# Queries and keys of batches 1 to 3: head-pair loads and 32x32 VectorE transposes in place of 64-column loads, TensorE and DMA transposes

## The chip, the cores and the metric

The kernel runs on one core of one Trainium2 chip. The metric is the device time of one execution in microseconds (us), lower is better; the figure compared is the median of several runs.

## What is computed

Four batches, 8 heads, 768 tokens, head size 64. Each chunk of 32 query tokens sees 8 memory keys and a window of up to 56 keys (16 before, its own 32, 8 after). The attention output, with heads joined to 512 columns, goes through a gated feed-forward layer of width 1536.

```python
for c in range(nc):                              # 24 chunks of 32 tokens
    q_c   = q[:, :, c_start:c_end]
    k_ctx = k[:, :, l_start:r_end]; v_ctx = v[:, :, l_start:r_end]
    k_full = np.concatenate([mem_k, k_ctx], axis=2)
    v_full = np.concatenate([mem_v, v_ctx], axis=2)
    scores = scale * np.matmul(q_c, k_full.transpose(0, 1, 3, 2))
    a = softmax(scores)                          # row maximum taken off first
    out[:, :, c_start:c_end] = np.matmul(a, v_full)
x = out.transpose(0, 2, 1, 3).reshape(3072, 512)
y = (np.maximum(x @ w_gate, 0) * (x @ w_val)) @ w_out
```

## The kernel before, in words

The work is cut into 24 tiles `a` of 128 tokens (six per batch). A tile needs its queries `qT` and its batch's keys `kT` with the head dimension on the partitions. `scores` (L286) makes one 64-column score block for each head and chunk; `row_max`, `subtract`, `row_sum`, `reciprocal`, `normalise` run on VectorE (DVE) and `exponent` on ScalarE (ACT); the weights are transposed (`p_t`, L343, on TensorE; from tile 18 on by a DMA transpose, L351), multiplied with the values (`values`, L357) and copied into `xT` (`x_copy`). The feed-forward layer runs over blocks of 2 or 4 tiles (`BLOCKS`, L51): `first` (L390) makes a gate and a value product for each of 12 slices of the width, `relu` (ACT) and `gate` (DVE) join them, `second` (L416) multiplies with the output weights and `store` writes out.

Queries and keys arrive in three ways. Batch 0 is loaded by `load_pair` (two tokens a descriptor) and transposed on TensorE (`pair_t`, L221; `pair_copy`). Tiles 6 to 11 are loaded by `load_qk` (L239: 128 tokens on the partitions, runs of 64 numbers), transposed on TensorE by `qk_t` (L260) and copied out by `qk_copy`. Tiles 12 to 23 (`LATE_QK`, L55) are loaded the same way and transposed by a DMA that SyncE (SP) issues, `qk_transfer` (L266): queries straight into `qT`, keys into `k_t`, from where `qk_copy` spreads them into `kT`. Values of batches 1 to 3 go into `v_bd` by `load_v_rows` (L170), and the memory rows by `mem_rows` (L152), all cast on the way by DMAs that GpSimd (POOL) issues.

The order of the instructions on each engine is fixed when the kernel is built: every operation has a key, a cost per engine, dependencies, a priority and the buffers it takes and gives (`room`), and `schedule` (L649) plays the engines through once, gives each engine the first ready operation by priority and emits them in that order. Feed-forward matmuls have the last priority and fill TensorE; `pace` (L145) holds the attention of a tile back until the feed-forward work has come to a given slice. Loads go out in the order of the list `loads` on POOL. Of the eight PSUM banks the feed-forward tiles and the value shifts take four (`fps`), a score tile two (`sps`), and all transposes and value products share two (`aps`).

Of the kernel before, what the change touches and what calls it, by code (L numbers as in the profile page):

```python
# [9 lines left out]
F32 = mybir.dt.float32  # L10
# [9 lines left out]
def kernel(  # L20
# [30 lines left out]
    BLOCKS = [2, 2, 4, 4, 4, 4, 4]  # L51
    GROUPS = [(0, 2), (2, 6), (6, 9), (9, 12)]
    BAND0 = 48

    LATE_QK, LATE_P = 12, 18  # L55
# [5 lines left out]
    ldpool = ctx.enter_context(tc.tile_pool(name="ldpool", bufs=18))  # L61
# [4 lines left out]
    ktpool = ctx.enter_context(tc.tile_pool(name="ktpool", bufs=3))  # L66
# [3 lines left out]
    fps = ctx.enter_context(tc.tile_pool(name="fps", bufs=4, space=bass.MemoryType.PSUM))  # L70
    sps = ctx.enter_context(tc.tile_pool(name="sps", bufs=1, space=bass.MemoryType.PSUM))
    aps = ctx.enter_context(tc.tile_pool(name="aps", bufs=2, space=bass.MemoryType.PSUM))
# [25 lines left out]
    v_n = {}  # L98
    qk_p = {(i, r): const.tile([128, H, 2 * D], BF16, name=f"qk_p_{i}_{r}") for i in range(2) for r in range(TPB // 2)}
# [40 lines left out]
    def mem_keys_t():  # L140
        TMP["kmem"] = aps.tile([128, B * HP * NMEM], F32, tag="aps", name="kmem_ps")
        nc.tensor.transpose(TMP["kmem"], kmem_f.rearrange("p a d -> p (a d)"), ident_f)
# [43 lines left out]
    def load_v_tile(t):  # L186
        v_n[t] = ldpool.tile([128, H, D], F16, tag="qk_b", name="v_n")
        nc.gpsimd.dma_start(
            v_n[t],
            bass.AP(tensor=v.tensor, offset=v[0, 0, 128 * t, 0].offset,  # L190
                    ap=[[D, 128], [S * D, H], [1, D]]))
# [29 lines left out]
    def pair_t(r, i, j):  # L221
        ps = TMP["pair", r, i, j] = aps.tile([128, HP, 128], BF16, tag="aps", name="qk_ps")
        for h in range(H):
            p = D * (h % 2)
            nc.tensor.transpose(ps[p:p + D, h // 2, :], qk_p[i, r][:, h, D * j:D * j + D], ident_b)  # L225
# [13 lines left out]
    def load_qk(a, i):  # L239
        b, t = divmod(a, TPB)  # L240
        x = (q, k)[i]
        qk_b[a, i] = ldpool.tile([128, H, D], BF16, tag="qk_b", name="qk_b")
        nc.gpsimd.dma_start(  # L243
            qk_b[a, i],
            bass.AP(tensor=x.tensor, offset=x[b, 0, 128 * t, 0].offset,
                    ap=[[D, 128], [S * D, H], [1, D]]))

    def new_batch(b):
        qT[b] = kvpool.tile([128, HP, S], BF16, name="qT")
        kT[b] = kvpool.tile([128, HP, NCH, KW], BF16, name="kT")  # L250
        src = kmemT[:, b]
# [3 lines left out]
                    ap=[src.ap[0], [NMEM, HP], [0, NCH], [1, NMEM]]))  # L255
# [4 lines left out]
    def qk_t(a, i):  # L260
        ps = TMP["qk", a, i] = aps.tile([128, HP, 128], BF16, tag="aps", name="qk_ps")
        x = qk_b.pop((a, i))
        for hp in range(HP):
            nc.tensor.transpose(ps[:, hp, :], x[:, 2 * hp:2 * hp + 2, :].rearrange("p h d -> p (h d)"), ident_b)  # L264

    def qk_transfer(a, i):  # L266
        b, t = divmod(a, TPB)
        if i == 0:
            o = qT[b][:, :, 128 * t:128 * t + 128]
        else:  # L270
            o = TMP["qk", a, i] = ktpool.tile([128, HP, 128], BF16, name="k_t")
        nc.sync.dma_start(o, qk_b.pop((a, i)).rearrange("p h d -> p (h d)"), transpose=True)

    def qk_copy(a, i, eng):
        b, t = divmod(a, TPB)
        ps = TMP.pop(("qk", a, i))
        if i == 0:
            copy(eng, qT[b][:, :, 128 * t:128 * t + 128], ps)
        else:
            o = kT[b][:, :, 4 * t:4 * t + 4, :]  # L280
            copy(eng,
                 bass.AP(tensor=o.tensor, offset=o.offset,
                         ap=[o.ap[0], [NCH * KW, HP], [KW, 4], [16 + NMEM, 2], [1, 16]]),
                 ps.rearrange("p h (c x s) -> p h c x s", c=4, x=2))

    def scores(a):  # L286
        b, t = divmod(a, TPB)
        s = sps.tile([128, 2, 512], F32, name="s_ps")
        keys = kT[b].rearrange("p h c s -> p h (c s)")
        for h2 in range(HP):  # L290
            m, par = h2 % 2, h2 // 2
            for g in range(4):
                c = 4 * t + g
                lo, hi = max(KW * c - 16, 0), min(KW * c + 48, NCH * KW)
                o0 = 64 * (2 * m + par) + lo - (KW * c - 16)
                for r in range(2):
                    d = slice(D * r, D * r + D)
                    nc.tensor.matmul(s[CH * g:CH * g + CH, r, o0:o0 + hi - lo],  # L298
                                     lhsT=qT[b][d, h2, CH * c:CH * c + CH],
                                     rhs=keys[d, h2, lo:hi], start=True, stop=True)  # L300
        S_ps[a] = s.rearrange("p a (h s) -> p a h s", s=64)[:, :, 0:HP, :]

    def row_max(a):
# [6 lines left out]
        SM[a, "mx"] = smpool.tile([128, 2, HP], F32, name="mx")  # L310
        nc.vector.reduce_max(SM[a, "mx"], s4, axis=AX.X)  # L311

    def subtract(a):
        mx = SM.pop((a, "mx"))
        SM[a, "dif"] = smpool.tile([128, HP, 2, 64], F32, name="dif")
        mx_b = bass.AP(tensor=mx.tensor, offset=mx.offset,
                       ap=[mx.ap[0], [HP, 2], [2, 2], [1, 2], [0, 64]])
        nc.vector.tensor_tensor(out=SM[a, "dif"].rearrange("p (m r) a s -> p r m a s", r=2),  # L318
                                in0=S_ps.pop(a).rearrange("p r (m a) s -> p r m a s", a=2),
                                in1=mx_b, op=ALU.subtract)  # L320
# [103 lines left out]
    def store(blk, t, c, eng):  # L424
# [12 lines left out]
    room = {"aps": 2, "sps": 1, "fps": 4, "mx": 2, "dif": 2, "p": 2, "sm": 2, "rinv": 2, "pn": 3, "kt": 3, "pT": 6,  # L437
            "qk": 18, "xT": 2, "gv": 2, "gr": 3, "o": 3, "kv": 2}
# [11 lines left out]
    def psum16(n):  # L450
# [8 lines left out]
    op("vmem_f", {"DVE": 0.55}, lambda e: nc.vector.memset(vmem_f, 0.0), prio=(-8,), after=["warm"])  # L459
    op("kml", {"SP": 1.4}, lambda e: mem_load(), prio=(-9,))  # L460
# [3 lines left out]
    op("kmt", {"PE": 0.25}, lambda e: mem_keys_t(), [("kml", 1.8), "if"], prio=(-5,), take=["aps"])  # L464
    op("kmc", {"ACT": 0.35}, lambda e: nc.scalar.copy(kmemT.rearrange("p b h m -> p (b h m)"), TMP.pop("kmem")),
       ["kmt"], prio=(-5,), give=["aps"])
    op("vm0", {"DVE": 0.5}, lambda e: nc.vector.tensor_copy(vmem_0, vmem_f), [("vml", 1.8)], prio=(-3,))
    for b in range(B):
        op(("new", b), {"DVE": 0.4}, lambda e, b=b: new_batch(b), ["kmc"], take=["kv"],
           prio=(-4.5,) if b == 0 else (1, TPB * b - 2, 0), after=[("t", TPB * b - 2, 0)] if b else [])  # L470


    AHEAD = 4

    def pace(a):
        blk = block_of[a]
        m = NDC * (a - starts[blk]) // BLOCKS[blk] - (AHEAD if a >= LATE_P else 0)
        if blk < 2:
            return []
        return [("f", blk - 1, m, 0)] if m >= 0 else [("f", blk - 2, m + NDC, 0)]  # L480


    ISSUE, LAND, SLACK, LAND_P = 1.4, 6.0, 8.0, 3.0

    def pace_t(a):
        return [("s", a - 4)]

    for a in range(NT):
        b, t = divmod(a, TPB)
        last = t == TPB - 1  # L490
        for i in (1, 0):
            if b == 0:
                if t % 2 == 0:
                    for j in range(2):
                        op(("t", a + j, i), {"PE": 0.3}, lambda e, a=a, i=i, j=j: pair_t(a // 2, i, j),
                           [("pl", a // 2, i), "ib", ("new", b)], (1, a - i, -2 + j), ["aps"])
                        op(("tc", a + j, i), psum16(HP * 128), lambda e, a=a, i=i, j=j: pair_copy(a // 2, i, j, engine[e]),
                           [("t", a + j, i)], (1, a - i, -2 + j), (), ["aps"])
                continue
            if a >= LATE_QK:  # L500
                op(("t", a, i), {"SP": ISSUE}, lambda e, a=a, i=i: qk_transfer(a, i),
                   [(("qk", a, i), SLACK), ("new", b)],
                   (1, a - i, 0), ["kt"] if i else [], [("qk", LAND)], pace_t(a))
                if i:
                    op(("tc", a, i), {"DVE": (0.2, 0.29), "ACT": (0.52, 0.62)}, lambda e, a=a, i=i: qk_copy(a, i, engine[e]),
                       [(("t", a, i), LAND)], (1, a - i, 0), (), ["kt"])
                continue
            op(("t", a, i), {"PE": 0.24}, lambda e, a=a, i=i: qk_t(a, i), [("qk", a, i), "ib", ("new", b)],
               (1, a - i, 0), ["aps"], ["qk"], pace(max(a - i, 0)))
            op(("tc", a, i), psum16(HP * 128), lambda e, a=a, i=i: qk_copy(a, i, engine[e]), [("t", a, i)],  # L510
               (1, a - i, 0), (), ["aps"])
        op(("s", a), {"PE": 0.36}, lambda e, a=a: scores(a),
           [(("t", a, 0), LAND) if a >= LATE_QK else ("tc", a, 0), ("tc", a, 1)]
           + ([] if last else [("tc", a + 1, 1)] if b or t % 2 == 0 else [("tc", a + 1, 1), ("tc", a + 2, 1)])
           + ([("tc", a ^ 1, 0)] if b == 0 else []), (1, a, 1), ["sps"],
           ["kv"] if last else [], [("s", a - 1)] if a else [])
# [13 lines left out]
        if b == 0:  # L530
            for c0 in (4 * t, 4 * t + 2):
                need = {c // 4 for c in (c0, c0 + 1)} | {max(c0 - 1, 0) // 4, min(c0 + 2, NCH - 1) // 4}
                gone = ([t - 1] if c0 % 4 == 0 and t else []) + ([t] if c0 == NCH - 2 else [])
                op(("sh", c0), {"PE": 0.4}, lambda e, c0=c0: shift(c0), [("vn", n) for n in sorted(need)] + ["ident"],
                   (1, a, 7.5), ["fps"], ["qk"] * len(gone), [("s", t)])
# [13 lines left out]
    seq = [(blk, m) for g0, g1 in GROUPS for blk in range(2) for m in range(g0, g1)]  # L549
    seq += [(0, None), (1, None)]  # L550
    for blk in range(2, len(BLOCKS)):
# [228 lines left out]
```

## Time and profile before

| | |
|---|---|
| median of 3 runs | 251.47 us (249.82 to 252.72) |
| the profiled execution | 254.24 us, of which the span of the instructions is 252.5 us |
| TensorE (PE) busy | 234.0 us, 93% of the span; mean granted clock 0.986 |
| VectorE / ScalarE / GpSimd busy | 131.3 / 115.0 / 90.7 us |
| chain that ended last | PE 79%, DMA 12%, DVE 4%, ACT 3% |
| DMA packets | 116285, of them 107297 under 512 B |

The profile is one execution of the program, taken by the hardware profiler. A line of a group names the source line, the engine, the operation, what is written and read, how often, and the busy time. A line of the timeline or of the chain gives start and length in us; a bracket at its end gives the idle time of that engine ahead of the instruction and what ended it. The time of an execution is a little longer than the span (1.7 us here), for what lies ahead of the first and behind the last instruction.

### The profile page before, as it was taken

What the parts mean: (1) busy time and instruction counts of PE and PEld (TensorE: products, weight loads), DVE (VectorE), ACT (ScalarE), POOL (GpSimd) and SP (SyncE); (2) the same over time, 40 slices, a digit from 0 to 9 for tenths busy, and PEclk for the clock granted to TensorE, in tenths of its full rate; (3) what the DMA queues carried; (4) which work ended last, traced back from release to release, by engine and by line L of the source; (5) the groups of instructions that cost most, each with busy time, mean ns of one, the idle gap of its engine ahead of it and who ended that gap; (6) DMA issues with size and microseconds to landing.
All of it is one profiled execution on the core that took longest, in us unless ns stands there. A gap on an engine that the chain in (4) does not pass through costs nothing.

```text
span 252.5 us, 6081 instructions
## 1 busy us (share of the span) xinstructions
PE 234.0 (93%) x2529; PEld 128.7 (51%) x2529; DVE 131.3 (52%) x245; ACT 115.0 (46%) x250; POOL 90.7 (36%) x105
## 2 busy tenths in 40 slices
PE   1869999999899999799999949999999999999994
PEld 0647887884445555345444424455444544444443
DVE  2462657985158886588543817964049340133400
ACT  2856757763236555356334444543153531333212
POOL 8975899605179950298450060000000000000000
PEclk9999999999999999999999976999999999999999
DMA  7999999999999999999999999222221101300022
GB/s 79 174 179 203 201 84 130 204 156 97 176 203 139 140 135 86 123 211 136 123 116 123 122 138 169 42 44 41 86 83 23 21 0 54 116 1 0 0 85 84
DMA packets 116285, 27.32 MB, mean 108 GB/s; under 512 B 107297, under 2 KB 113185, under 8 KB 116257
## 3 DMA queue, kind: packets, MB, share of 16 engines
q0 software_dynamic: 94368, 16.42, 113.4%
q1 hardware_dynamic: 21888, 10.51, 24.3%
q8 instruction: 20, 0.33, 0.6%
q14 instruction: 9, 0.07, 0.1%
HBM read 32.06 MB, written 6.29 MB: 152 GB/s over the span
## 4 chain that ended last, share of the span: by engine, by line
PE 79%; DMA 12%; DVE 4%; ACT 3%; issue 1%; POOL 0%; SPq 0%; ACTq 0%; POOLq 0%
PE v_ps L396 25%; PE g_ps L396 25%; PE out_ps L421 18%; DMA k_t<-qk_b 9%; PE s_ps L298 2%; PE xT_ps L377 2%; DMA qk_p<-in_q_dram 2%; PE xT_ps L370 2%; PE vs_ps L204 1%; PE qk_ps L225 1%; PE pT_ps L347 1%; DVE mx L311 1%; DVE dif L318 1%; PE qk_ps L264 1%; PE xT_ps L363 1%
## 5 line engine op out<-in xcount | busy, mean ns | idle before, releaser
L408 DVE TENSOR_TENSOR gvT<-v_ps,g_relu 128x512 f16<-128x512 f32 (+1 forms) x84 | 51.3, 611 | 51.9 <-PE v_ps L396 48.9
L396 PE MATMUL g_ps<-xT,w_gate_sb 128*128 128x512 f16 (+1 forms) x336 | 77.4, 353 | 0.8 <-ACT xT L78 0.8
L396 PE MATMUL v_ps<-xT,w_val_sb 128*128 128x512 f16 (+1 forms) x336 | 77.8, 355 | 0.0
L402 ACT ACTIVATE g_relu<-g_ps 128x512 f16<-128x512 f32 (+1 forms) x84 | 45.0, 535 | 56.2 <-PE g_ps L396 55.9
L421 PE MATMUL out_ps<-w_out_sb,gvT 128*128 128x512 f16 (+2 forms) x300 | 64.9, 371 | 0.0
L396 PEld LDWEIGHTS <-w_gate_sb 128*128 128x128 f16 x336 | 31.7, 99 | 28.3 <-issue 2.0
L396 PEld LDWEIGHTS <-w_val_sb 128*128 128x128 f16 x336 | 31.7, 99 | 27.2 <-issue 1.5
L421 PEld LDWEIGHTS <-gvT 128*128 128x128 f16 x300 | 28.2, 98 | 31.3
L78 ACT COPY o_sb<-out_ps 128x512 f32<-128x512 f32 (+2 forms) x25 | 14.1, 565 | 36.4 <-PE out_ps L421 32.5
L311 DVE TENSOR_REDUCE mx<-s_ps 128x8 f32<-128x512 f32 x24 | 16.4, 683 | 18.7 <-PE s_ps L298 18.2
L326 ACT ACTIVATE p_exp<-dif 128x256 f16<-128x256 f32 (+2 forms) x72 | 19.6, 336 | 10.7 <-DVE dif L318 10.5
L243 POOL DMA_DIRECT2D qk_b<-in_k_dram x18 | 16.4, 911 | 14.4 <-issue 8.0
L330 DVE TENSOR_REDUCE sm<-p_exp 128x8 f32<-128x512 f16 x24 | 16.3, 681 | 9.2 <-ACT p_exp L326 9.0
L156 POOL DMA_DIRECT2D v_bd<-vmem x16 | 10.1, 637 | 28.6 <-DMA v_bd<-in_v_dram 27.4
L243 POOL DMA_DIRECT2D qk_b<-in_q_dram x18 | 16.4, 909 | 3.8 <-issue 2.5
L341 DVE TENSOR_TENSOR p_n<-p_exp,rinv 128x512 f16<-128x512 f16 x24 | 16.5, 687 | 0.4
L318 DVE TENSOR_TENSOR dif<-s_ps,mx 128x512 f32<-128x512 f32 x24 | 16.5, 686 | 0.4
L173 POOL DMA_DIRECT2D v_bd<-in_v_dram x7 | 13.9, 1996 | 5.2 <-issue 3.7
L298 PE MATMUL s_ps<-kT,qT 64*32 64x64 bf16 (+2 forms) x768 | 8.6, 199 | 5.7 <-ACT kT L78 3.3
L298 PEld LDWEIGHTS <-qT 64*32 64x32 bf16 x768 | 5.3, 92 | 14.0 <-issue 11.8
L78 ACT CAST xT<-xT_ps 128x512 f16<-128x512 f32 x14 | 8.2, 586 | 8.5 <-PE xT_ps L377 4.5
L377 PEld LDWEIGHTS <-v_bd 128*128 128x128 f16 x288 | 9.4, 97 | 3.6 <-issue 0.3
(52 smaller groups left out, 159.8 us busy)
## 6 DMA issues: line engine op xcount, KB each, us to landing
out_dram<-o_sb SPq DMA_DIRECT2D x23, 256.0 KB
v_bd<-in_v_dram POOLq DMA_DIRECT2D x5, 672.0 KB, 18.0
qk_b<-in_k_dram POOLq DMA_DIRECT2D x18, 128.0 KB, 7.5
qk_b<-in_q_dram POOLq DMA_DIRECT2D x18, 128.0 KB, 7.8
w_out_sb<-in_moe_w_out_dram POOLq DMA_DIRECT2D x2, 768.0 KB, 11.6
qk_p<-in_k_dram POOLq DMA_DIRECT2D x3, 256.0 KB, 6.1
qk_p<-in_q_dram POOLq DMA_DIRECT2D x3, 256.0 KB, 6.5
v_n<-in_v_dram POOLq DMA_DIRECT2D x6, 128.0 KB, 6.5
```

The lines of the kernel that those rows point to most:

```text
L78: nc.scalar.copy(o, i)
L243: nc.gpsimd.dma_start(qk_b[a, i], bass.AP(tensor=x.tensor, offset=x[b, 0, 128 * t, 0].offset, ap=[[D, 128], [S * D, H], [1, D]]))
L298: nc.tensor.matmul(s[CH * g:CH * g + CH, r, o0:o0 + hi - lo], lhsT=qT[b][d, h2, CH * c:CH * c + CH], rhs=keys[d, h2, lo:hi], start=True, s ...
L311: nc.vector.reduce_max(SM[a, "mx"], s4, axis=AX.X)
L318: nc.vector.tensor_tensor(out=SM[a, "dif"].rearrange("p (m r) a s -> p r m a s", r=2), in0=S_ps.pop(a).rearrange("p r (m a) s -> p r m a s ...
L326: nc.scalar.activation(p[:, :, :, s0:s0 + k1 - k0], dif[:, :, :, k0:k1], ACT.Exp, scale=SCALE)
L330: nc.vector.reduce_sum(SM[a, "sm"], SM[a, "p"], axis=AX.X)
L341: nc.vector.tensor_tensor(out=P_n[a], in0=SM.pop((a, "p")), in1=rinv_b, op=ALU.mult)
L396: nc.tensor.matmul(ps, lhsT=w[:, f, 128 * m:128 * m + 128], rhs=xTs[blk][:, f, :], start=(f == 0), stop=(f == NFC - 1))
L402: nc.scalar.activation(st["r", m], st.pop((0, m)), ACT.Relu)
L408: nc.vector.tensor_tensor(out=st["gv"][:, m, :], in0=st.pop((1, m)), in1=st.pop(("r", m)), op=ALU.mult)
L421: nc.tensor.matmul(st["o", t, c], lhsT=st["gv"][:, m, 128 * t:128 * t + 128], rhs=w_out_sb[:, m, c[0]:c[1]], start=(m == 0), stop=(m == ND ...
```

## The change

Batch 0 keeps its way. For batches 1 to 3:

- Loads. Per batch, query or key: four DMAs of 384 descriptors (one for each pair of heads, onto 32 partitions) in place of six of 1024; a descriptor reads four tokens, 256 numbers. They sit in whole-batch buffers, three of them, one shared with batch 0's values.
- Transposes. Per batch eight `keys_t` (128 partitions, 384 elements each) and six `queries_t` (512 elements) on DVE, in 32x32 blocks, straight into `kT` and `qT`. The TensorE transposes and copies of tiles 6 to 11, the 24 DMA transposes and the copies from `k_t` are gone.
- Head halves. A head's 64 numbers now lie as two halves of 32 on the same partitions, so `scores` makes two accumulating products of 32 rows for each head and chunk: 64 matmuls a tile in place of 32, each head pair into a PSUM bank of its own. Memory keys of batches 1 to 3 are loaded apart (four small DMAs), zero-filled and transposed on DVE once (`mem_keys_b`).
- PSUM. Scores take four banks (batch 0 uses the upper two for its transposes), feed-forward three (before four), weight transposes and value products one (before two).
- Blocks. [2, 2, 2, 4, 4, 4, 4, 2] in place of [2, 2, 4, 4, 4, 4, 4].
- Order. `pace` works from an estimated clock; the last group of gate weights is loaded behind the last query pair and value tile of batch 0; two of the four zero fills of `v_bd[1]` move from POOL to DVE ahead of everything else; key and query loads of batch 1 stand behind the output weights, and those of batches 2 and 3 behind the values of the batch before.

```diff
-    BLOCKS = [2, 2, 4, 4, 4, 4, 4]
+    BLOCKS = [2, 2, 2, 4, 4, 4, 4, 2]
-    ldpool = ctx.enter_context(tc.tile_pool(name="ldpool", bufs=18))
+    ldpool = ctx.enter_context(tc.tile_pool(name="ldpool", bufs=3))
-    fps = ctx.enter_context(tc.tile_pool(name="fps", bufs=4, space=bass.MemoryType.PSUM))
+    fps = ctx.enter_context(tc.tile_pool(name="fps", bufs=3, space=bass.MemoryType.PSUM))
-    aps = ctx.enter_context(tc.tile_pool(name="aps", bufs=2, space=bass.MemoryType.PSUM))
+    aps = ctx.enter_context(tc.tile_pool(name="aps", bufs=1, space=bass.MemoryType.PSUM))
+    s_all = sps.tile([128, 4, 512], F32, name="s_ps")
...
-        nc.gpsimd.dma_start(
-            qk_b[a, i],
-            bass.AP(tensor=x.tensor, offset=x[b, 0, 128 * t, 0].offset,
-                    ap=[[D, 128], [S * D, H], [1, D]]))
+        nc.gpsimd.dma_start(
+            qk_b[b, i][CH * hg:CH * hg + CH],
+            bass.AP(tensor=x.tensor, offset=x[b, 2 * hg, 0, 0].offset,
+                    ap=[[TPP * D, CH], [128 * D, 2 * TPB], [1, TPP * D]]))
...
+    def queries_t(b, r, h):
+        n = TPB * h + 2 * r
+        o = qT[b][:, 2 * h, 256 * r:256 * r + 256]
+        nc.vector.transpose(
+            bass.AP(tensor=o.tensor, offset=o.offset, ap=[o.ap[0], [128, 2], [1, TPP], [S, 2], [TPP, CH]]),
+            qk_b[b, 0][:, n:n + 2].rearrange("p n j d -> p (n j d)"))
+
+    def keys_t(b, j, e):
+        o = kT[b][:, e, :, j:KW]
+        nc.vector.transpose(
+            bass.AP(tensor=o.tensor, offset=o.offset,
+                    ap=[o.ap[0], [2 * NCH * KW, 2], [KW, NCH], [16 + NMEM, 2], [TPP, 16 // TPP]]),
+            qk_b[b, 1][:, :, j, CH * e:CH * e + CH])
...
-    def qk_transfer(a, i):
-        nc.sync.dma_start(o, qk_b.pop((a, i)).rearrange("p h d -> p (h d)"), transpose=True)
...
+        S_ps[a] = s_all[:, :, 0:128].rearrange("p g (h s) -> p g h s", s=64)
+        for h in range(2):
+            for e in range(2):
+                for hg in range(4):
+                    d = slice(CH * hg, CH * hg + CH)
+                    for g in range(4):
...
+                        nc.tensor.matmul(s_all[CH * g:CH * g + CH, hg, o0:o0 + hi - lo],
+                                         lhsT=qT[b][d, 2 * h + e, CH * c:CH * c + CH],
+                                         rhs=keys[d, 2 * h + e, lo:hi], start=(e == 0), stop=(e == 1))
...
+    for hp in range(2):
+        op(("z", 1, hp), {"DVE": 1.7}, lambda e, hp=hp: zero(nc.vector, v_bd[1], hp), prio=(-7.5, hp), after=["vmem_f"])
...
+    for hg in range(4):
+        load(("mk", hg), 208, 0.2, lambda hg=hg: mem_keys(hg), ["kmb0"])
     for i in range(2):
         load(("wo", i), 768, 4.1, lambda i=i: load_out(i))
+    load_qk_op(1, 1)
+    load_qk_op(1, 0)
```

## The prediction

> **What bounds the kernel now.** I read the page first, for shares; then the chain that ended last, for where time passes that is no matrix work; then the timeline around those places, for prices.
>
> ```profile
> PE 234.0 (93%) x2529; PEld 128.7 (51%) x2529; DVE 131.3 (52%) x245; ACT 115.0 (46%) x250; POOL 90.7 (36%) x105
> ...
> PE 79%; DMA 12%; DVE 4%; ACT 3%; issue 1%; POOL 0%; SPq 0%; ACTq 0%; POOLq 0%
> ```
>
> TensorE is the bound, with little left: 18.5 us of the span without a matmul. About 9 of them lie in the first 20 us (loads and the first softmax) and 3.3 behind the last matmul. What the change aims at is most of the rest, waits for keys that a DMA transposes. The chain around 140 us, columns start, length, what:
>
> ```profile
> 136.70 12.23 DMA k_t<-qk_b
> ...
> 148.95 0.63 ACT kT L78
> ...
> 149.62 0.39 PE s_ps L298 x22
> 150.01 1.82 PE v_ps L396 x4
> 151.83 1.71 PE g_ps L396 x4
> 153.54 0.43 PE xT_ps L377 x16
> 153.97 1.62 PE v_ps L396 x4
> ```
>
> One key transpose takes 12.2 us to land, its copy ends at 149.58, and only then do the scores go on. Afterwards three feed-forward groups take 1.82, 1.71 and 1.62 us where the usual one takes 0.86: the clock had fallen.
>
> ```profile
> 150.00:160.00 10.00, 10.00 (x111) 4.07 (x111) 8.25 (x16) 5.92 (x16) 0.00 (x0) 0.73 1.19 126
> ```
>
> In this stretch the granted clock (third from the end) is 0.73, DVE busy 8.25 of 10. The timeline gives the idle time ahead of the scores (in brackets) there and at two earlier places:
>
> ```profile
> 107.39 0.29 PE L298 MATMUL s_ps<-kT,qT 64*32 64x64 bf16 x26 [1.54 <-DVE kT L80]
> ...
> 110.69 0.32 PE L298 MATMUL s_ps<-kT,qT 64*32 64x64 bf16 x32 [0.49 <-DVE dif L318]
> ```
> ```profile
> 149.62 0.39 PE L298 MATMUL s_ps<-kT,qT 64*32 64x64 bf16 x26 [3.35 <-ACT kT L78]
> ```
>
> **The change, part by part.** The sum is made against the profiled execution, 254.24 us (span 252.5 and 1.7 around it). It lies 2.8 above the median of 251.47; the difference found below is taken off the median.
>
> *Waits on DMA transposes: gone.* 1.54 + 0.49 + 3.35 = 5.4 us idle, and at the lower clock 0.96 + 0.85 + 0.76 = 2.6 us: -8.0. What is late next is under landing, below. The other executions may not all pay the 2.6, so the gain against the median may be 5.4.
>
> *TensorE transposes of tiles 6 to 11: gone.* Twelve groups of four; one stands between groups that start at 89.42 and 89.65, so 0.23 us each: -2.8. Their PSUM copies go too (ACT 6 qT and kT copies at about 0.6 each are off the path).
>
> *Scores of 18 tiles: 64 matmuls in place of 32.* A block of 32 now lasts 0.31 us with matmuls of 0.19, so its starts span 0.12 us, 3.9 ns apart; 0.24 us pass until the next group starts. [...] Upper bound: the starts stay 3.9 ns apart, 64 need 0.25, and 18 x 0.12 = +2.2. I take +2.2, since 3.9 is the only distance that the trace shows. [...]
>
> *One more block of two.* Groups with 256 columns start 0.435 us apart (48.44 to 48.88), with 512 0.86: 48 more of the former against 24 fewer of the latter, 20.9 - 20.7 = +0.2. Twelve more relu and gate pairs (0.39 and 0.42 us) lie beside matmuls.
>
> *DVE.* Added: 24 `keys_t` of 384 elements and 18 `queries_t` of 512. The trace shows no such operation. Nearest rows: a 16-bit SBUF copy of 512 elements 0.29 us (lower), a tensor operation on 512 at full length 0.69, one every 0.60 (upper, keys by size 0.47). I take the upper, since a transpose streams one element after another like those: 24 x 0.47 + 18 x 0.60 = 22 us. With two zero fills (1.6 each from 0.485 for 512), a zero fill of 1024 (1.0) and one transpose, less some ten copies, DVE rises from 131 to about 155 us. [...]
> Does it fit? In the emitted order the key transposes of each batch stand mostly where TensorE multiplies with the output weights (5 to 10 us without a gate). Adding DVE's starts between successive gates, no stretch needs over 1.3 us more on DVE than on TensorE. But feed-forward has three PSUM banks, not four. A value product's bank is free about 0.17 + 0.69 us after its end, while the product that needs it starts one group (0.86) and a half behind: some 0.8 us of slack where there was 1.7, about one DVE operation of 0.69 or one tile's three exponentials (0.81). Some of the 48 gates that fall beside attention will meet both. I take ten times 0.15 us, +1.5 (bounds 0, if the order always fits; +6, if one gate in four loses 0.5 us).
>
> *One bank for weight transposes and value products* makes transposing, copying, multiplying, copying of a tile a chain of 0.23 + 0.6 + 0.4 + 0.7 = 1.9 us against 7.4 us between tiles: hidden by feed-forward groups, except in the start.
>
> *Start.* Scores of tiles 2 and 3 and two value shifts (12 matmuls, 1.49 us at the low clock) move ahead of the first feed-forward group, into idle times of 1.43 and 0.67 us; that is work done earlier, but the second value product waits for the first's copy (+0.6). The zero fills on DVE end at about 4.7, so the first memory-key transpose starts 0.8 later, still ahead of the first keys at 6.1. Together 0 (bounds -2, if the clock rises sooner, +2).
>
> *Landing.* POOL saves two fills of 1.34 us. On its queue, memory keys (four issues at about 0.65), output weights, then eight loads of batch 1 and the values follow. An output weight half (0.75 MB) landed every 3.7 us (49.8 and 53.5); batch 1's keys, as many bytes, stand right behind both. From about 38 us: 43, 47, keys 51, queries 55, values 69 (before: 67.0). The first `keys_t` stands on DVE behind the gate of the 22nd of 24 small slices, by the order 49 to 51 us; what waits behind it are the last three gates, and TensorE behind these. The queries are needed by about 56, the values at some 71 (before, the product stood at 67.66, just behind their landing). Likewise the memory-key transpose holds the gates behind it if its loads land after 37.8 (I get 37 to 39). I take +1.5 (bounds 0 and +5). Batches 2 and 3 are ahead: 36 loads of 1024 descriptors become 24 of 384, so the queue carries some 27000 packets fewer of its 94368.
>
> Sum: -8.0 - 2.8 + 2.2 + 0.2 + 1.5 + 1.5 = -5.4, or 248.8 for such an execution and 246.1 for the median. Since the median may lack part of the 2.6, I give 246.5.
>
> **Rivals.**
> *A. The order doesn't fit DVE (slower).* If a transpose costs twice what I took (0.94 and 1.2, a reason could be that it writes in steps of four tokens), DVE has 22 us more. The eight key transposes then last 7.5 us and outlast the output stretch of 5.2; the gates behind them come late and three banks give no cover. Following the order, TensorE loses about 5 us at 1.5 times the price and 14 at twice: -5.4 + 14 = +8.6, 260. It is slower than before from about 1.5 times on. For it: DVE is already busy 8.7 of 10 in dense stretches. Against it: full-length operations on this engine all sit at 0.60 to 0.69.
> *B. Batch 1 lands late.* If the loads need as long as those issued at 45 us in the trace of before (22 us), keys land at 59 and TensorE stands some 6 us more, with a clock that falls again (2.6): 246.5 + 7 = 253, no change. For: DMA engines are at 9 tenths in all slices up to 158 us. Against: in the trace that was behind 1.3 MB of short value runs, here it is ahead of them.
> [...]
> *D. The waits were hidden anyway.* If other executions pay only half of them, -1 to -2: 250.
>
> **How the numbers follow.** Forecast (243 to 249): 0.45. C: 0.15. D: 0.12. B: 0.13. A: 0.15, half of it beyond 256. A measurement of this kernel can tell about 1%, here 2.5 us. Faster by over 1% (under 249): 0.45 + 0.15 and a little of D, 0.62. Within 1%: D and half of B, 0.18. Slower: A and the rest of B, 0.20. The range reaches from C's upper end, 240.5, to between B and A, 256; the likeliest case alone 243 to 249.
>
> **What would show it.** Right: no key transposes on SP, no idle above 1 us ahead of the scores between 75 and 170 us, granted clock near 1.00 throughout, transposes on DVE at 0.55 and 0.69 us, a score block's starts 0.25 us long. Wrong: idle of DVE ahead of its first `keys_t` or memory-key transpose (landing), feed-forward matmuls waiting for DVE or ACT (banks), transposes above 0.8 us (A), or an end of the first two blocks later than 57 us (start).

## The result

| kernel | median, us | range, us | runs | ratio to before (95%) |
|---|---|---|---|---|
| before | 252.09 | 249.82 to 252.72 | 4 | |
| after | 263.37 | 262.58 to 265.94 | 4 | 1.048 (1.038 to 1.059) |

The change makes the kernel 11 us slower; 246.5 was forecast, with 256 as the upper end. In the profiled execution (265.94 us, span 264.2) TensorE is busy 238.1 us and idle 26.1, where it was 234.0 and 18.5 before. The table of the experiments gives medians without the executions that took over 1.5% longer than the fastest of the same kernel; the profiled executions of before, e5, e7 and e12 are such longer ones.

The page of after, its shares, the chain that ended last, and two groups (busy us, mean ns of one):

```profile
PE 238.1 (90%) x3153; PEld 141.2 (53%) x3153; DVE 171.1 (65%) x294; ACT 109.3 (41%) x247; POOL 73.5 (28%) x95
...
PE 77%; DVE 15%; issue 4%; ACT 2%; DMA 2%; DVEq 0%; POOLq 0%
...
L281 DVE STREAM_TRANSPOSE qT<-qk_b 128x512 bf16<-128x512 bf16 x18 | 22.7, 1315 | 0.0
L287 DVE STREAM_TRANSPOSE kT<-qk_b 128x384 bf16<-128x384 bf16 x24 | 22.1, 1034 | 0.0
```

DMA has left the chain (12% to 2%), as meant; DVE has taken its place (4% to 15%). The 42 transposes need 44.8 us, where 22 were forecast. The groups of DVE by shape hold a third kind of transpose, the one of the memory keys, whose destination is plain:

```profile
L258 DVE STREAM_TRANSPOSE kmem<-qk_p 128x512 bf16<-128x512 bf16 x1 | 0.7, 702 | 0.0
```

The same 512 elements take 0.702 us there and 1.315 where every fourth element is written. The waits of TensorE, by what ended them (us in total, times, longest):

```profile
PE s_ps L323 <- issue: 3.9, 2, 2.4
PE g_ps L427 <- DVE gvT L439: 3.0, 5, 0.9
PE s_ps L323 <- DVE qT L281: 2.1, 2, 1.2
PE s_ps L235 <- ACT kT L78: 1.4, 1, 1.4
PE s_ps L235 <- ACT qT L78: 1.4, 1, 1.4
PE s_ps L235 <- DVE dif L343: 1.4, 1, 1.4
```

None of these was in the trace of before at such a size. Three kinds are to be told apart: waits for DVE (second, third row), waits inside score blocks for nothing that the profile shows (first), and waits of the pair transposes at the start (the last three). The stretch from 150 us, shown for before with a clock of 0.73, now has the full clock and a full DVE (columns behind the time: length, TensorE, weight loads, DVE, ScalarE, GpSimd, each with its instructions, clock, DMA share, GB/s):

```profile
150.00:160.00 10.00, 8.02 (x115) 3.92 (x114) 10.00 (x15) 3.34 (x6) 0.00 (x0) 1.00 0.01 2
```

DVE is busy 10.00 of 10 us and TensorE 8.02. The chain there:

```profile
152.40 1.04 DVE kT L287
153.44 0.46 DVE gvT L439
153.90 2.46 DVE kT L287 x3
156.36 0.03 issue
156.40 0.72 DVE gvT L439
157.11 1.79 DVE kT L287 x2
```

Between two gates stand one to three key transposes; the gate that frees a feed-forward bank comes when they are done.

Last, a score block and the group behind it, from the timelines of before and of after:

```profile
91.47 0.31 PE L298 MATMUL s_ps<-kT,qT 64*32 64x64 bf16 x32
91.71 0.40 PE L347 MATMUL pT_ps<-band,p_n 128*128 128x128 f16 x4
```
```profile
99.71 0.68 PE L323 MATMUL s_ps<-kT,qT 32*32 32x64 bf16 x64
100.32 1.04 PE L427 MATMUL v_ps<-xT,w_val_sb 128*128 128x512 f16 x4
```

The next group starts 0.61 us behind the block's start; before, with 32 matmuls, it was 0.24. That is 0.37 us a tile, three times the 0.12 of the forecast. The records of the single matmuls of this block of after show where it goes: the first 31 start 3.3 ns apart, then 0.12 us pass with one more start in it, and from the 33rd on they start 8.3 ns apart, 0.48 us from the first start to the last.

### The profile page after: what moved, and what is told of

It reads as the page before. It is cut to its first block, busy times and chain, and to the rows that moved or that the text cites. A ratio compares the mean times of both kernels' runs of the same rounds, so it can differ in the third digit from the quotient of the medians.

```text
span 264.2 us, 7340 instructions
## 1 busy us (share of the span) xinstructions
PE 238.1 (90%) x3153; PEld 141.2 (53%) x3153; DVE 171.1 (65%) x294; ACT 109.3 (41%) x247; POOL 73.5 (28%) x95
## 4 chain that ended last, share of the span: by engine, by line
PE 77%; DVE 15%; issue 4%; ACT 2%; DMA 2%; DVEq 0%; POOLq 0%
PE out_ps L452 21%; PE g_ps L427 21%; PE v_ps L427 20%; DVE kT L287 4%; DVE qT L281 4%; PE s_ps L323 3%; PE xT_ps L408 3%; DVE gvT L439 2%; PE s_ps L235 2%; DMA qk_p<-in_k_dram 2%; PE pT_ps L378 2%; PE vs_ps L214 2%; DVE mx L335 1%; PE xT_ps L401 1%; ACT kT L78 1%
## 5 line engine op out<-in xcount | busy, mean ns | idle before, releaser
L439 DVE TENSOR_TENSOR gvT<-v_ps,g_relu 128x256 f16<-128x256 f32 (+1 forms) x96 | 53.4, 557 | 47.5 <-PE v_ps L427 33.7
L427 PE MATMUL g_ps<-xT,w_gate_sb 128*128 128x256 f16 (+1 forms) x384 | 78.5, 327 | 3.2 <-DVE gvT L439 3.0
L427 PE MATMUL v_ps<-xT,w_val_sb 128*128 128x256 f16 (+1 forms) x384 | 78.6, 327 | 0.0
L433 ACT ACTIVATE g_relu<-g_ps 128x256 f16<-128x256 f32 (+1 forms) x96 | 47.0, 489 | 65.0 <-PE g_ps L427 64.8
L427 PEld LDWEIGHTS <-w_gate_sb 128*128 128x128 f16 x384 | 36.6, 98 | 29.9 <-issue 6.1
L281 DVE STREAM_TRANSPOSE qT<-qk_b 128x512 bf16<-128x512 bf16 x18 | 22.7, 1315 | 0.0
L287 DVE STREAM_TRANSPOSE kT<-qk_b 128x384 bf16<-128x384 bf16 x24 | 22.1, 1034 | 0.0
L323 PE MATMUL s_ps<-kT,qT 32*32 32x64 bf16 (+2 forms) x1152 | 12.4, 196 | 7.0 <-issue 3.9
L323 PEld LDWEIGHTS <-qT 32*32 32x32 bf16 x1152 | 9.9, 87 | 14.3 <-issue 10.6
L264 POOL DMA_DIRECT2D qk_b<-in_q_dram x12 | 7.3, 612 | 21.1 <-DMA v_bd<-in_v_dram 8.6
```

The costliest lines, as they stand in the source:

```text
L281: nc.vector.transpose(bass.AP(tensor=o.tensor, offset=o.offset, ap=[o.ap[0], [128, 2], [1, TPP], [S, 2], [TPP, CH]]), qk_b[b, 0][:, n:n + ...
L287: nc.vector.transpose(bass.AP(tensor=o.tensor, offset=o.offset, ap=[o.ap[0], [2 * NCH * KW, 2], [KW, NCH], [16 + NMEM, 2], [TPP, 16 // TPP]]),
L323: nc.tensor.matmul(s_all[CH * g:CH * g + CH, hg, o0:o0 + hi - lo], lhsT=qT[b][d, 2 * h + e, CH * c:CH * c + CH], rhs=keys[d, 2 * h + e, lo ...
L427: nc.tensor.matmul(ps, lhsT=w[:, f, 128 * m:128 * m + 128], rhs=xTs[blk][:, f, :], start=(f == 0), stop=(f == NFC - 1))
L433: nc.scalar.activation(st["r", m], st.pop((0, m)), ACT.Relu)
L439: nc.vector.tensor_tensor(out=st["gv"][:, m, :], in0=st.pop((1, m)), in1=st.pop(("r", m)), op=ALU.mult)
```

## Experiments

Theory: three parts of the change cost time. The transposes write in steps of four tokens, at twice the price (my rival A); the second half of the scores costs 0.37 us a tile and more; scores and pair transposes of batch 0 are cut from one PSUM tile, and wait for one another. Rivals: the transposes were hidden, and scores and start are all; or the planner's order is at fault, which was made with half of the price; or the waits for DMA transposes were no loss.

| run | median, us | before beside it | ratio to before (95%) |
|---|---|---|---|
| e1_runs_of_8 | 257.50 | 251.67 | 1.021 (1.008 to 1.034) |
| e2_half_scores | 259.50 | 251.67 | 1.029 (1.019 to 1.040) |
| e3_own_banks | 260.65 | 251.67 | 1.036 (1.024 to 1.048) |
| e4_before_all_pe | 251.96 | 251.67 | 1.001 (0.997 to 1.005) |
| e5_halves_apart | 261.96 | 251.55 | 1.040 (1.033 to 1.047) |
| e6_three_undone | 245.88 | 251.55 | 0.975 (0.969 to 0.982) |
| e7_best | 257.14 | 251.55 | 1.019 (1.012 to 1.025) |
| e8_one_issue | 250.87 | 251.31 | 0.999 (0.994 to 1.003) |
| e9_true_costs | 264.55 | 251.31 | 1.054 (1.046 to 1.062) |
| e10_batch1_pe | 252.49 | 251.42 | 1.002 (0.999 to 1.006) |
| e11_copy_on_act | 247.40 | 250.54 | 0.988 (0.983 to 0.994) |
| e12_price_and_start | 254.85 | 252.30 | 1.011 (1.003 to 1.019) |

**The price of a transpose.**

```
-  ap=[o.ap[0], [128, 2], [1, TPP], [S, 2], [TPP, CH]])            # queries
+  ap=[o.ap[0], [128, 2], [CH, TPP], [S, 2], [1, CH]])
-  ap=[o.ap[0], [2*NCH*KW, 2], [KW, NCH], [16+NMEM, 2], [TPP, 4]]) # keys, offset j
+  ap=[o.ap[0], [2*NCH*KW, 2], [KW, NCH], [1, 8]])                 # offset (0, 8, 24, 32)[j]
```

> The changed kernel, with the same instructions in the same order; the 42 transposes of batches 1 to 3 write runs of adjacent elements (8 for keys, 32 for queries) where the changed kernel writes every fourth element. Tokens stand in another order inside a chunk (keys) and inside 128 tokens (queries), so this kernel computes attention with permuted tokens. Theory W (the price of a transpose is set by how it writes): 384 and 512 elements take about 0.55 and 0.70 us, as the one transpose with a plain destination (0.702 us for 512), in place of 1.034 and 1.315; DVE's busy time falls by 24 x 0.48 + 18 x 0.61 = 22 us, the idle times of TensorE behind query transposes (1.23 and 0.82 us near 65 us, 3.0 us ahead of g_ps, 2.3 near 150 to 170) shrink, and the time falls by 4 to 6 us from 263.4, to 257.5 to 259.5. Rival P (the price belongs to reading the loaded tiles, or the transposes were hidden and the loss lies in scores and start): durations unchanged, or changed with less than 1.5 us in the time: 262 or more.

Measured: 257.50, 5.9 us less than after. Page of this kernel:

```profile
L287 DVE STREAM_TRANSPOSE kT<-qk_b 128x384 bf16<-128x384 bf16 x24 | 12.1, 549 | 0.0
L281 DVE STREAM_TRANSPOSE qT<-qk_b 128x512 bf16<-128x512 bf16 x18 | 12.0, 687 | 0.0
```

With the same source, order and length the price halves when adjacent elements are written (1.034 to 0.549 us, 1.315 to 0.687). Theory W holds: the waits for gates (3.0) and for query transposes (2.1) are gone from the list, the 3.9 inside blocks stay (4.1).

**Scores.**

```
-            for e in range(2):
+            for e in range(1):
...
-                         start=(e == 0), stop=(e == 1))
+                         start=True, stop=True)
```

> The changed kernel with only the first of the two 32-row halves of the scores of batches 1 to 3 (32 matmuls a tile in place of 64), so scores lack half of the head's dimensions. Theory S (the second half costs what the trace shows): a block of 64 holds TensorE 0.61 us until the next group starts where 32 held it 0.24; without the second half about 0.24 to 0.30, 18 x 0.31 to 0.37 = 5.6 to 6.7 us less, and perhaps part of the 3.9 us of waits inside blocks that no releaser explains: 253 to 258. Rival L (the forecast's own term, 18 x 0.12 = 2.2 us, with the rest hidden in waits for other engines): 260 to 262.

Measured: 259.50, 3.9 us less, between the two. A block goes back to 0.24 us:

```profile
96.01 0.31 PE L323 MATMUL s_ps<-kT,qT 32*32 32x64 bf16 x32
96.25 1.04 PE L427 MATMUL v_ps<-xT,w_val_sb 128*128 128x512 f16 x4
```

So 32 matmuls of 32 rows cost TensorE as much as 32 of 64 rows did (0.24 us), and the waits inside blocks are gone. But its waits for gates rise:

```profile
PE g_ps L427 <- DVE gvT L439: 4.6, 7, 0.9
```

4.6 us in place of 3.0: a faster TensorE met the same full DVE. What scores really cost could not be read while the transposes were slow; e6 and e12 settle it.

**The start.**

```
-    s_all = sps.tile([128, 4, 512], F32, name="s_ps")
+    S_bank = [sps0.tile([128, 2, 512], F32, name="s_ps")]
+    spares = [sps0.tile([128, 512], F32, name=f"qk_ps_{i}") for i in range(2)]
...
+        if a == TPB:
+            begin.close()
+            S_bank[0] = sps.tile([128, 4, 512], F32, name="s_ps")
```

> The changed kernel with the same order of instructions; in batch 0 the scores and the two banks for pair transposes are three PSUM tiles of their own, given back before the four-bank tile is made for batch 1, where the changed kernel cuts them all from one four-bank tile. Theory T (waits at the start come from sharing that tile: 1.41 us ahead of the transposes at 8.79, 1.41 at 11.26 and 1.39 at 14.84, the last for the subtraction of scores in another bank): the first probability transpose comes some 2 to 3 us sooner than 18.89, and the time falls by 2 to 3.5 us, to 260 to 261.5. Rival Z (the zero fills on DVE and the memory cast ahead of the first copy set the start): first scores stay near 11.8, and the time within 1 us of 263.4.

Measured: 260.65, 2.7 us less. Pair transposes and probability transpose in its timeline:

```profile
7.67 1.19 PE L237 MATMUL qk_ps<-ident_b,qk_p 128*64 128x128 bf16 x16 [0.45 <-DMA qk_p<-in_q_dram]
9.22 0.64 PE L237 MATMUL qk_ps<-ident_b,qk_p 128*64 128x128 bf16 x8 [0.36 <-DMA qk_p<-in_k_dram]
...
15.56 0.61 PE L385 MATMUL pT_ps<-band,p_n 128*128 128x128 f16 x4 [0.90 <-DVE p_n L379]
```

In after these stand at 8.79, 11.26 and 18.89, the first two behind waits of 1.41 for copies out of other banks of the tile. The zero fills on DVE are the same in both kernels, so theory T holds against Z. In this profile the waits inside blocks are also shorter (0.3 in place of 3.9; more on them at the end of the next section); the same edit made on top of e1 (e12 against e1) gives 2.65, so most of the gain is not theirs.

**The waits that the change was to remove.**

```
-    LATE_QK, LATE_P = 12, 18
+    LATE_QK, LATE_P = 24, 18
```

> The kernel before with all transposes of keys and queries on TensorE, none by DMA (its border between the two moved from tile 12 behind the last tile): the first term of the forecast by itself. Theory G (the waits for DMA transposes and the low clock behind them cost what was read, 8.0 us, or 5.4 without the clock): 24 groups more at 0.23 us are +5.5, so 252.1 - 8.0 + 5.5 = 249.6, or 252.2 without the clock's part; no idle over 1 us ahead of scores after 75 us. Rival D (the waits were hidden anyway, another wait takes their place): 252.1 + 5.5 - 1 = 256 to 258.

Measured: 251.96, level with before (1.001). After the first 20 us no wait ahead of scores over 0.2 us is left in its profile. With 5.5 us of added transposes (24 groups of 0.23, an estimate) the waits were worth 5.2 us by the ratio, 4.2 to 6.2 by its interval: that is the idle part of the forecast's term, 5.4, without the 2.6 of the clock, and rival D (256 to 258) falls.

**Why the second half of the scores is slow.**

```
-        for h in range(2):
-            for e in range(2):
+        for e in range(2):
+            for h in range(2):
```

> The changed kernel with the two 32-row halves of the scores of batches 1 to 3 further apart: the loop over halves is the outermost, so that a matmul that adds to a result follows 32 matmuls behind the one that began it, in place of 16. Theory Q (the second half is slow because it waits for the first: one matmul lasts 196 ns, 16 of them start within about 62 to 120 ns): a block of 64, which holds TensorE 0.61 us until the next group starts, falls to about 0.48, twice the 0.24 of 32; 18 x 0.13 = 2.3 us less, 261. Rival R (64 matmuls with 64 weight loads need that long, whatever their order): 0.61 as before, 263.4 within 1 us.

Measured: 261.96. The time alone, 1.4 us under after, does not separate the theories; the block does, which still holds TensorE as long:

```profile
100.34 0.68 PE L323 MATMUL s_ps<-kT,qT 32*32 32x64 bf16 x64
100.96 0.60 PE L428 MATMUL v_ps<-xT,w_val_sb 128*128 128x512 f16 x2
```

0.62 us, where 0.48 was expected, and 0.68 from the first start to the last end, as in after. Theory Q falls: it is not the distance between a result's two halves.

**All three, and two of three.** e6 joins the edits of e1, e2 and e3; e12 joins those of e1 and e3 and keeps all 64 matmuls.

> The changed kernel with all three edits at once: transposes that write adjacent elements (tokens permuted), only the first half of the scores' rows (half of the head's dimensions left out), PSUM tiles of its own for batch 0. Theory X (in the run with half the scores, the slow transposes took back what the scores gave: feed-forward products waited 4.6 us for gates in place of 3.0, and for subtractions): the three together give more than the sum of the single runs, 5.8 + 2.7 + 6.7 of score time and the 3.9 of unexplained waits in blocks: 244 to 248. Rival Y (the three are independent): 263.4 - 5.8 - 3.9 - 2.7 = 251.

> The changed kernel with transposes that write adjacent elements (tokens permuted) and PSUM tiles of its own for batch 0, and with all 64 score matmuls a tile: against the run with all three edits (245.9) it gives the price of the doubled scores when DVE is not in the way. Theory X (with slow transposes DVE hid part of the scores' cost, 3.9 of some 10 us): scores now cost 18 x 0.37 = 6.7 and about 2 to 4 us of waits inside blocks: 254.5 to 256.5. Rival Y2 (the scores' cost is 3.9 us in any company, and it is the two other edits that help each other): 249 to 251.

Measured: 245.88 and 254.85. Theory X holds in both. The four kernels make a ladder, one edit a step: 245.9 (e6), +9.0 with the second half of the scores 254.9 (e12), +5.8 with the strided write 260.7 (e3), +2.7 with the shared tile 263.4 (after). Each rung is the median of three or four executions, which spread over 0.6 us (e6) to 3.4 us (after), so a step can be off by one to two. Of the 9.0, 18 x 0.37 = 6.7 are block time; the other 2.3 are of the size of the waits inside blocks, of which e6's profile has none. In e12's:

```profile
PE s_ps L330 <- issue: 3.1, 2, 1.6
PE v_ps L434 <- DVE gvT L446: 2.6, 1, 2.6
```

The second row is a late landing: DVE idled 4.8 us there ahead of its first key transpose at 54.98. With slow transposes the same half of the scores was worth 3.9 (e2).

**The order.** Three costs in the planner:

```
-  {"DVE": (0.47, 0.55)}  (0.6, 0.68)   {"PE": 0.3 if b else 0.36}
+  {"DVE": (0.95, 1.03)}  (1.23, 1.31)  {"PE": 0.61 if b else 0.36}
```

> The changed kernel with three costs of its planner set to what the trace shows (keys 0.95, queries 1.23, a score block of batches 1 to 3 0.61 us, in place of 0.47, 0.60 and 0.30); the instructions are the same, their order is planned anew. Theory O (the slow transposes hurt because the order was made for fast ones): feed-forward products no longer wait for gates (3.0 us) and part of the 3.0 near 65 us goes; 259 to 261. Rival N (the time of DVE itself is missing where the transposes lie, in any order): 262.5 to 264.

Measured: 264.55, nothing gained (rival N, a little above its range). The waits moved: gates no longer delay g_ps, but a copy of the values' result that now stands on DVE does.

```profile
PE g_ps L427 <- DVE xT L80: 2.5, 2, 1.8
```

**A version built from this.** The transposes were fast where they wrote adjacent elements (0.549 and 0.687 us in e1), and 32 matmuls cover a tile's scores only if each contracts 64 rows. Both are to be had: each half of a head's dimensions goes to its own group of 32 partitions, which costs loading everything twice, and strides move from the write of the transpose to reads.

```
+        o = qk_b[b, i][CH*hg:CH*hg + CH, CH*(1 - e):CH*(1 - e) + NG*TPP*D]   # r, e = divmod(hg, 2)
+   keys:    ap=[o.ap[0], [KW, 2 * NCH], [16 + NMEM, 2], [8, 2], [1, 2]]       # runs of two
+   queries: ap=[o.ap[0], [S, HP], [8, TPP], [CH, 4], [1, 8]]                  # runs of eight
+   scores:  rhs ap=[rhs.ap[0], [8, (hi - lo) // 8], [1, 2], [2, TPP]]
+   xT copy: x ap=[x.ap[0], [128, NFC], [CH, 4], [1, 8], [8, TPP]]
```

> A version built from what the runs show, computing all of the reference. Batches 1 to 3: each group of 32 partitions loads four heads of its row half's parity (twice the bytes, the odd groups shifted by 32 elements), so that a 32x32 transpose puts one half of the head's dimensions into each group and the scores contract 64 rows in 32 matmuls and two banks, as before the change; transposes write runs of 2 (keys) and 8 (queries) adjacent elements, the scores' moving operand reads the keys in order, the copy of the values' result undoes the order of the queries; four feed-forward banks and two for the small products, as before the change. Theory V (the loss of the change is the price of the strided write, the doubled scores and the shared tile): keys about 0.55 us and queries 0.70, score blocks 0.24, start as before (first scores about 9.7): 245 to 249, under the kernel before. Rival W (a run of two elements, four bytes, is still a strided write, or doubled loads of batch 1 land late): keys stay near 1.0 us, or DVE idles ahead of the first keys after 56 us; 252 to 256.

Measured: 257.14, slower than both ranges. Half of it as theory V has it: transposes 0.549 and 0.693 us (a run of two elements is enough), score blocks 0.24.

```profile
L281 DVE STREAM_TRANSPOSE kT<-qk_b 128x384 bf16<-128x384 bf16 x24 | 12.0, 549 | 2.5 <-DMA qk_b<-in_k_dram 2.5
L275 DVE STREAM_TRANSPOSE qT<-qk_b 128x512 bf16<-128x512 bf16 x18 | 12.2, 693 | 9.8 <-DMA qk_b<-in_q_dram 9.4 <-issue 0.4
```

But GpSimd issued the last queries of batch 1 at 63.9 us, and TensorE waited 6.0 us for them and 3.3 for repeated memory rows of batch 2 (W, as to the loads).

```
-        for h2 in range(HP):                       # four loads, x[b, 2 * h2 + r]
+        nc.gpsimd.dma_start(..., x[b, HP * r], ap=[[TPP*D, CH], [128*D, NG], [1, TPP*D]])
```

> The built version again, with heads dealt to the row halves so that the four heads of a half lie side by side in memory: one load per group of 32 partitions in place of four, 24 issues on GpSimd in place of 96, the same bytes. Theory V2 (only the loads' queue spoiled the first try: GpSimd held the queries of batch 1 until 64 us, and at most eight transfers were under way): no wait of 6 us ahead of the first scores of batch 1, none for the repeated memory rows of batch 2, so 257.9 - 6.0 - 3.3 = 248 to 250. Rival W2 (the doubled bytes themselves come too late for batch 1): queries of batch 1 after 62 us, 2 to 4 us of wait left, 251 to 254.

Measured: 250.87, level with before. The last queries were issued at 46.6 us, and yet:

```profile
70.29 0.41 PE L304 MATMUL s_ps<-kT,qT 64*32 64x48 bf16 x32 [5.84 <-DVE qT L274]
```

The bytes themselves are late: DVE idles 6.15 us for them, until 69.52 (W2, with a longer wait than its 2 to 4 us); only the second wait went with the issues. So batch 1 goes back to loads by tiles and TensorE:

```
+  for a, i in late[:5]: load_tile_op(a, i)      # [128 tokens, heads, 64], once
+  op(("t", a, i), {"PE": 0.24}, ... tile_t(a, i) ...)   # batch 1 only
```

> The built version with keys and queries of batch 1 loaded by tiles, once, and transposed on TensorE as before the change (12 groups of 0.23 us); batches 2 and 3 keep the doubled loads and the transposes on DVE in runs of two and eight. Theory V3 (all that held the second try at the level of the kernel before is the doubled bytes of batch 1, 5.8 us of wait and about 1 us of low clock behind it): 250.9 - 6.8 + 2.8 = 246 to 248, 1.5 to 2.5% under the kernel before. Rival U (the loads of batch 1 by tiles take their place in the queue and values or the keys of batch 2 come late instead): a wait of 2 us or more between 60 and 120 us; 249 to 252.

Measured: 252.49, level with before again; rival U. One wait (1.9 us, put down to a key load by the profile) ends as the values of batch 1 land, ahead of the first product with them; the other is this, DVE first, then GpSimd and TensorE:

```profile
81.56 3.95 DVE L295 COPY kT<-kmemT 128x768 bf16<-128x768 bf16 x1
```
```profile
79.73 5.36 POOL L140 MEMSET v_bd<- 128x1536 f32 x4
```
```profile
86.48 1.01 PE L434 MATMUL g_ps<-xT,w_gate_sb 128*128 128x256 f16 x4 [2.35 <-DVE gvT L446]
```

A copy that takes 0.34 to 0.54 us elsewhere in this kernel begins in the middle of GpSimd's zero fills and ends 0.4 us behind them; four matmuls of 256 columns then take 1.01 us where they took 0.60.

```
-        op(("new", b), {"DVE": 0.4}, lambda e, b=b: new_batch(b), ...)
+        op(("new", b), {"ACT": (0.74, 0.85)} if b else {"DVE": 0.4}, lambda e, b=b: new_batch(b, engine[e]), ...)
```

> The kernel of the run before with one edit: the copy of the memory keys into the key tiles of batches 1 to 3 goes from DVE to ScalarE. In that run the copy lasted 3.95 us in batch 2, where it takes 0.35 elsewhere; it began at 81.56, in the middle of GpSimd's zero fills (79.73 to 85.09), and ended 0.4 us behind them, as another did in the run with three edits (1.73 us, ended 0.2 behind the fills). Gates queued behind it let TensorE wait 2.35 us, and its clock was at half for some 8 us afterwards. [...] Rival H (another wait is next in the same stretch: gates, or the queue of loads): 250 to 252.

Measured: 247.40, 0.988 (0.983 to 0.994) of before and under rival H's range; no wait for a gate is left in the list of TensorE's waits. This is the one version here that computes all of the reference and is faster than both kernels, if by 1.2% only. The copy takes 0.84 us on ScalarE from 75.39 on, ahead of the fills (78.75 to 84.20). From 80 to 90 us TensorE is busy throughout at full clock:

```profile
80.00:90.00 10.00, 10.00 (x96) 6.42 (x95) 5.27 (x12) 4.01 (x11) 9.70 (x8) 1.00 1.41 188
```

In e10 it was busy 7.64 us there with a clock of 0.83, and the clock was 1.00 from 90 to 100: half the clock for about 3.4 us, by an estimate from the 0.83, and not for the 8 of the expectation.

## Why the prediction was wrong

Three terms of the sum failed. Against the forecast of 246.5 the scores are short by 6.8 us (9.0 in place of 2.2), the DVE term by 5.8 and the start by 2.7; the 1.6 that are left to the measured 263.4 are all the other terms together.

1. **The DVE term: the price of a transpose.** "I take the upper, since a transpose streams one element after another like those": 0.47 and 0.60 us. Measured 1.034 and 1.315. The upper end of my bounds came from operations that write plainly, and I let it bound one that writes in steps of eight bytes, though I named that step as a reason under rival A. The working was in reach: the added operations hold one plain and 42 strided transposes, and the nearest rows fit only the former (0.702). Theory W and e1 show it: 5.9 us alone, 5.8 on the ladder. Each further element took 1.1 ns where the writes were adjacent (e1) and 2.2 where every fourth element was written (after).
2. **Rival A was right in mechanism and in price (twice), and too large alone.** It gave +8.6 by 14 us of losses on TensorE; the strided write costs 5.8 to 5.9. That its 260 lies near the measured 263.4 is luck, since scores and start make up the rest. Its first place, eight key transposes outlasting the output stretch, took the form of waits for query transposes near 65 us (2.1); gates held by transposes cost 3.0 further on.
3. **Scores: +2.2 forecast, 9.0 measured** (e12 against e6), the largest of the three. The forecast let the time from the last start to the next group stand, and that held (0.12 us before, 0.13 after). What failed is "the starts stay 3.9 ns apart": that distance was read over 32 matmuls, and only the first 31 of the 64 keep to it (3.3); a pause and starts 8.3 ns apart follow, so that the starts span 0.48 us and not 0.25. This makes 6.7; the rest is waits inside blocks, which the trace of before hardly announced (0.2 us in all). That a second half costs nothing, as the lower end of the range (240.5) has it, no run shows: 64 matmuls hold TensorE 0.61 us where 32 hold it 0.24.
4. **Start: 0 forecast (-2 to +2), +2.7 measured** (e3), beyond the bound. I followed queues and zero fills and did not ask what shares a tile. The low clock that the forecast gives the value shifts there was read from their time alone: 12 matmuls take 1.49 us at 12.39 in before and 0.85 at 27.15, and the profile's clock is 1.00 in both stretches. The end of the first two blocks was the mark I had set: output matmuls begin at 59.87, behind the 57 us named.
5. **Waits for DMA transposes: -8.0 forecast, -5.2 by e4.** Right in kind and, as the forecast feared, without the clock's 2.6; the clock stayed near 1.00 in after, as foretold.
6. **Banks +1.5 and landing +1.5.** Banks: with fast transposes, half the scores and three feed-forward banks (e6) gates delay TensorE by 1.0 us in all; within the bounds. Landing: DVE was not idle ahead of its first key transpose at 55.98, so in after this term is nothing. The late start hides it, though: with batch 0 some 3 us sooner DVE idles 1.7 us for these keys in e6, without loss on TensorE, and 4.8 in e12's profile, where TensorE loses 2.6. The transposes that left TensorE (-2.8) were not measured by themselves.

With the three failed terms cured, the total comes out: the forecast without the second half of the scores is 246.5 - 2.2 = 244.3, and e6 takes 245.9. It is a total only; the waits gave 2.8 less than their -8.0, and banks and landing took less than their 3.0.

The cause of the waits inside blocks is not settled. A DMA queue that the profile calls `instruction` (q8) moves 24 packets of 16,384 bytes in after, where TensorE has 6306 weight loads and matmuls, and 20 in before, where it has 5058. The two waits end 1.52 and 1.58 us behind the end of one such packet each (74.70 and 80.83), and the two matmuls stand exactly 256 of TensorE's instructions apart. In e1 (2.54 and 1.57 us) and e5 (1.43 and 1.56) the same two matmuls wait, in e12 there are two such waits (3.1 us in all), in e3 only the second is left (0.27), and with 32 matmuls a tile (e2, e6) none is seen. That TensorE waited there for its own instructions is the author's reading of these places and times: no run changes the packets alone, and why these two would come late is not shown. Open, too, is the pause behind the 31st matmul of a block (0.12 us) and the 8.3 ns behind it; e5 only rules out the order of the halves.

The two matmuls' places in the timeline of after:

```profile
76.22 0.45 PE L323 MATMUL s_ps<-kT,qT 32*32 32x64 bf16 x37 [2.37 <-issue]
...
82.41 0.20 PE L323 MATMUL s_ps<-kT,qT 32*32 32x64 bf16 x3 [1.56 <-issue]
```

## What to carry to other kernels

Price an operation by a row with the same write pattern; where the trace has none, the bound must reach to a multiple of the plain price (1.9 times here), and try a stride on the side that reads, where it cost nothing here (0.585 us against 0.584 for the copy). A distance between starts that was read over 32 small matmuls (3.9 ns here) is a price for 32 and not for 64 (8.3 from the 33rd on); look at what a longer run of them does before it is doubled. Ask for every tile that is cut into parts who else holds a part. Where two costs fall on different engines in one stretch, removing one shows only what the other leaves visible (3.9 against 9.0 us here), so undo them together as well as singly.

## What the runs showed of the hardware

- A DVE transpose of 2-byte elements that writes every fourth element takes 1.034 us for 384 and 1.315 for 512 (after), 2.2 ns for each further element; in runs of 8 (384) and 32 (512) it takes 0.549 and 0.687 (e1), in runs of 2 and 8 0.549 and 0.693 (e7) or 0.544 and 0.692 (e8), about 1.1 ns each. A run of two was enough.
- Two strided reads cost nothing that can be seen: score blocks whose moving operand takes every second key still hold TensorE 0.24 us (e8), and the copies of the values' result that read PSUM in steps of eight take 0.585 us on ScalarE in e7, as the plain ones do in after (0.584).
- The copy of 768 elements on DVE that met GpSimd's zero fills in e10 took 3.95 us (81.56 to 85.51, the four fills 79.73 to 85.09), where it takes 0.34 to 0.54 elsewhere in that kernel; another in e6 took 1.73 (from 75.71) and ended 0.2 us behind the fills. At 1.34 us a fill, two further fills began, by estimate, while the copy of e10 ran. Three other DVE operations that began within these fills (80.24, 80.57, 81.21) took 0.41, 0.68 and 0.42 us. What held the copy is not shown: in e11 it stands on ScalarE and ahead of the fills.
- 32 matmuls that contract 32 rows (e2) hold TensorE as long as 32 that contract 64 (before), 0.24 us; 64 of them hold it 0.61 (after), with starts 3.3 ns apart for the first 31 and 8.3 ns apart from the 33rd on.
- TensorE stood 2.4 and 1.6 us inside score blocks of after, each time until 1.5 to 1.6 us behind the end of a 16,384-byte packet of the `instruction` queue, at matmuls 256 instructions apart.
